# Batch 0's stretch dealt in another order, its squares summed by TensorE, and one projection product moved ahead in the states' layer

## The chip, the cores and the metric

The kernel runs on one core of a Trainium2 chip. The metric is the device time of one launch in microseconds (us), here the median of three runs. Five engines of a core matter: TensorE (PE, with its weight loads PEld), VectorE (DVE), ScalarE (ACT), GpSimd (POOL) and SyncE (SP), which issues the transfers.

## The reference

```python
# x: (8, 8, 512, 64), state: (8, 8, 32, 64), per batch and head
a  = softmax(x @ state.T / 8)          # 512 x 32
xread = a @ state                      # 512 x 64, the tokens' read
a2 = softmax(state @ x.T / 8)          # 32 x 512
sread = a2 @ x                         # 32 x 64, the states' read
y  = concatenate([xread, sread])       # per batch 544 rows of 8 * 64 = 512
xn = y / sqrt(mean(y * y) + 1e-6) * rms_g
g, v = xn @ w_gate, xn @ w_val         # 512 -> 1536
out = (g * sigmoid(g) * v) @ w_out     # 1536 -> 512
```

Over all batches that makes 4096 token rows and 256 state rows. The computation is in 32-bit floats; the weights and `x` arrive as 64-bit values.

## The kernel before

**Stages.** Batch 0 is computed first, in a stretch of its own in which the weights are also converted. Batches 1 to 7 follow in a steady form. At the end the layer is run once more for the 256 state rows of all batches ("the states").

**Tokens and weights.** The tokens' read of a batch is not written out. Because a softmax over 32 states leaves 32 weights per token and head, the kernel keeps those weights (`aT_s`, 128 x 2 x 512) and folds the states into the layer's weights: `own_weights` multiplies the scaled states `stT_g` with `w_m` (gate and value weights) in L454, and ACT copies the result out of PSUM into `v` (L465). The hidden layer of batch 0 is then `aT_s` times `v` (L496), with Silu on ACT (L502) and the gate product on DVE (L506), and the projection is L694. Batches 1 to 7 and the states use a form with seven block products in place of eight (L600 in `hidden_seven`, L754 in `project_seven`), with sums on DVE and POOL.

**Root mean square.** `tokens_read` does compute the read once (L336), for its squares alone: ACT squares four PSUM banks into `sq` (L343), DVE adds the four (L346, three instructions), TensorE sums over the partitions with a vector of ones (L350, four matmuls of one column), DVE adds 1e-6 (`ss`, L354), POOL takes the power -1/2 (`ri`, L254), TensorE spreads it along the rows (L261), and DVE scales `aT_s` by it (L360). Only then can the hidden layer begin. The token softmax before that is on DVE and ACT: transpose L302, maximum L311, subtraction L313, exponential L315, sum, reciprocal and multiplication (L322 to L327), transpose L329. The state softmax and read, `states_read`, is maximum L372, scaling L375, exponential L378, transposes L385, products L397, scaling L404, transpose L408 and a copy into `xsT` (L410).

**Conversion.** The weights are cut into six groups `mp` of three pieces (gate, value, output). Each piece takes three steps on ACT, L199, L201 and L204 (stream `exponents`), and four on DVE, L225, L228, L232 and L237 (stream `values`). Their raw bits come through a ring of four buffers; the intermediate `ex` and `top` have two buffers each.

**What sets the order.** Every part is a generator. PE, DVE and ACT run in the order in which the generators are stepped; SP's transfers and POOL's work are placed by the scheduler. For batch 0's stretch that order is written out as a string, `ORDER`, one letter per step: `a` and `s` are the tokens' and states' read of batch 0, `A` and `S` those of batch 1, `e` and `d` the conversion, `v` the own weights, `h`, `t`, `u` the hidden products, Silu and gate products of batch 0, `p` and `c` its projection and copies out, `k` sums of the output weights, `w` the first own weights of batch 1, `z` a dummy matmul (`keep_awake`, L845). `PERIOD` does the same for batches 1 to 7, and `STATES` for the states. Inside `hidden_seven`, `sums` finishes each group `mp`: three additions (L662), then the gate (states: L671), then for the later groups a sum (L679) and a difference (L682) that `project_seven` needs.

**Buffers.** PSUM has two banks under the name `at`, two under `pv`, two, one and one for `fx`, `fy` and `fz`. The four reads of L336 take both `at` and both `pv` banks.

Of the kernel before, what the change touches and what calls it, by code (L numbers as in the profile page):

```python
# [8 lines left out]
F32 = mybir.dt.float32  # L9
# [3 lines left out]
ALU = mybir.AluOpType  # L13
# [4 lines left out]
P = 128  # L18
# [1 line left out]
W_BUFS = 3  # L20

ORDER = (
    "aaaaaaaaddaaaaaaeaseeaasadsasszzzzzzzzzzzzzzssdsaaaasaeadesaeeazzsdasaaezzzzzzza"
    "deadaaaddeeazzzzsedaadszzzzzadaeedzzvvavdzzadeaAzzzzhdeeddtdAdAAhueheAeedtddphAe"
    "dvdvduvdphedeAedtdhApeehddeuAdddeAhdedvdtudvvpeAAAAdhdAAteAehuhpddephepdeAdAeApA"
    "dteedAAvvveAdpudAAephtdSdhAdphdeAueedhAdeAteudddeeSppAddAAdppAdAdevApvdveehhAdth"
    "AudhpdeddeedeAdteAupvdvdvphedAAtdShhutSAhpukSSSkkkwSwkpSkpwpSSckSScckkpcSwkkkwww"
    "w"
)

PERIOD = (
# [4 lines left out]

STATES = (
    "hyyyyhthyytthhhuuhtuhththhytuuhuuhthuhhtthyuhyyutyhhhuuuttyuhhutyyhhthuhyhuhuttu"
    "yhuhttyuhuhuuhuthhyuthythytuhuuhuhutuuhuuppcpkpcpukkcpkpkpc"
)  # L40


# [1 line left out]
def kernel(  # L44
# [20 lines left out]
    VE, SE, GE, TE = nc.vector, nc.scalar, nc.gpsimd, nc.tensor  # L65
# [5 lines left out]
    NC = S // P  # L71
# [13 lines left out]
    aps = ctx.enter_context(tc.tile_pool(name="aps", bufs=2, space=PSUM))  # L85
# [4 lines left out]
    seven = {}  # L90
# [17 lines left out]
    def load_x(b, *queues):  # L108
        x_sb[b] = two.tile([P, NC, H * D], F32, name="x_b")
        for c in range(NC):  # L110
# [8 lines left out]
    ones = consts.tile([P, 1], F32, name="ones")  # L119
# [3 lines left out]
                     in0=ones.to_broadcast([P, NC]), op=ALU.pow)  # L123
# [9 lines left out]
    hb = consts.tile([P, NM, S], F32, name="hb")  # L133
# [133 lines left out]
    def tokens_read(b):  # L267
        xb, packed = x_sb[b], rows.pop(b)
        stT = two.tile([P, 4, Ns], F32, name="stT")
        stT_g[b] = two.tile([P, 4, Ns], F32, name="stT_g")  # L270
        tp = aps.tile([P, 4, Ns], F32, name="at")
        TE.transpose(out=tp.rearrange("p j n -> p (j n)"),
                     in_=packed.rearrange("p e d -> p (e d)"), identity=ident)
        yield
        VE.tensor_copy(stT, tp)
        yield "step"

        xT = one.tile([P, 4, NC, P], F32, name="xT", tag="xT")
        for c in range(NC):
            tp = aps.tile([P, 4, P], F32, name="at")  # L280
            for j in range(4):
                TE.transpose(out=tp[:, j, :], in_=xb[:, c, P * j:P * j + P], identity=ident)  # L282
            yield
            SE.copy(xT[:, :, c, :], tp)
            yield "step"


        sp = [aps.tile([P, S], F32, name="at") for e in range(2)]
        for j in range(4):
            for e in range(2):  # L290
                TE.matmul(out=sp[e][Ns * j:Ns * j + Ns, :], lhsT=stT[D * e:D * e + D, j, :],  # L291
                          rhs=xT[D * e:D * e + D, j].rearrange("p c t -> p (c t)"),
                          start=True, stop=True)
        yield


        sS = read[b] = two.tile([P, 2, NC, P], F32, name="sS")
        eS = one.tile([P, 2, S // Ns, Ns], F32, name="eS", tag="eS")
        m1 = two.tile([P, 2, S // Ns], F32, name="m1")
        z1 = two.tile([P, 2, S // Ns], F32, name="z1")  # L300
        for e in range(2):
            VE.transpose(out=eS[:, e].rearrange("p k n -> p (k n)"), in_=sp[e])  # L302
            yield
            SE.copy(sS[:, e].rearrange("p c t -> p (c t)"), sp[e])
            yield "step" if e else None

        def along(t, e):
            return t[:, e].unsqueeze(2).to_broadcast([P, S // Ns, Ns])

        for e in range(2):  # L310
            VE.reduce_max(out=m1[:, e], in_=eS[:, e], axis=AXX)  # L311
            yield
            VE.tensor_tensor(out=eS[:, e], in0=eS[:, e], in1=along(m1, e), op=ALU.subtract)  # L313
            yield
            SE.activation(out=eS[:, e], in_=eS[:, e], func=ACTF.Exp, scale=SCALE)  # L315
            yield "step"
        VE.tensor_tensor(out=stT_g[b], in0=stT, in1=rms_g.unsqueeze(2).to_broadcast([P, 4, Ns]),
                         op=ALU.mult)
        yield
        aT_s[b] = two.tile([P, 2, S], F32, name="aT_s")  # L320
        for e in range(2):
            VE.reduce_sum(out=z1[:, e], in_=eS[:, e], axis=AXX)  # L322
            yield
            VE.tensor_scalar(z1[:, e], z1[:, e], 1e-9, None, op0=ALU.add)
            VE.reciprocal(z1[:, e], z1[:, e])
            yield
            VE.tensor_tensor(out=eS[:, e], in0=eS[:, e], in1=along(z1, e), op=ALU.mult)  # L327
            yield
            VE.transpose(out=aT_s[b][:, e], in_=eS[:, e].rearrange("p k n -> p (k n)"))  # L329
            yield "step"  # L330


        reads = [(aps, vps)[j // 2].tile([P, S], F32, name=("at", "pv")[j // 2]) for j in range(4)]
        for j in range(4):
            for e in range(2):
                TE.matmul(out=reads[j][D * e:D * e + D, :],  # L336
                          lhsT=packed[Ns * j:Ns * j + Ns, e, :],
                          rhs=aT_s[b][Ns * j:Ns * j + Ns, e],
                          start=True, stop=True)
        yield  # L340
        sq = one.tile([P, 4, S], F32, name="sq", tag="xT")
        for i, j in enumerate((2, 3, 0, 1)):
            SE.activation(out=sq[:, i, :], in_=reads[j], func=ACTF.Square, scale=DM ** -0.5)  # L343
            yield "step" if i == 3 else None
        for i, j in ((0, 1), (2, 3), (0, 2)):
            VE.tensor_tensor(out=sq[:, i, :], in0=sq[:, i, :], in1=sq[:, j, :], op=ALU.add)  # L346
            yield
        sp = aps.tile([P, NC], F32, name="at")
        for c in range(NC):
            TE.matmul(out=sp[:, c:c + 1], lhsT=sq[:, 0, P * c:P * c + P], rhs=ones,  # L350
                      start=True, stop=True)
        yield
        ss = two.tile([P, NC], F32, name="ss")
        VE.tensor_scalar(ss, sp, 1e-6, None, op0=ALU.add)  # L354
        yield "step"
        ri = mean_root(ss, NC)
        yield
        rp = along_rows(ri, NC)
        yield
        VE.tensor_tensor(out=aT_s[b], in0=aT_s[b],  # L360
                         in1=rp.unsqueeze(1).to_broadcast([P, 2, S]), op=ALU.mult)
        yield "step"
# [75 lines left out]
    HM = NM // 2  # L438
# [151 lines left out]
    def hidden_seven(n, weights, tokens, silu, after=lambda mp: None):  # L590
# [67 lines left out]
        def sums():  # L658
            for mp, q in enumerate(pairs):
                h = hb[:, 2 * mp:2 * mp + 2, 0:n]  # L660
                for to, ps in ((gates(q)[1], "z"), (gates(q)[0], "y"), (q["c"], "x")):
                    VE.tensor_tensor(out=to, in0=to, in1=q[ps][:, :, 0:half], op=ALU.add)  # L662
                    yield
                if not silu:
                    VE.scalar_tensor_tensor(out=h, in0=h, scalar=1.0, op0=ALU.add, op1=ALU.mult,  # L665
                                            in1=q["g"].rearrange("p m c t -> p m (c t)"))
                    yield
                for i, val in ((1, q["c"]), (0, q["x"][:, :, 0:half])):
                    part = h[:, :, half * i:half * i + half]
                    if silu:  # L670
                        VE.tensor_tensor(out=part, in0=part, in1=val, op=ALU.mult)  # L671
                    else:
                        VE.scalar_tensor_tensor(out=part, in0=part, scalar=0.5, in1=val,
                                                op0=ALU.mult, op1=ALU.mult)
                    yield
                if 2 * mp >= HM:
                    k = 2 * mp - HM
                    upper, lower = (hb[:, k:k + 2, half * i:half * i + half] for i in range(2))
                    VE.tensor_tensor(out=seven["s"][:, k:k + 2, 0:half], in0=lower,  # L679
                                     in1=h[:, :, half:n], op=ALU.add)  # L680
                    yield
                    VE.tensor_tensor(out=lower, in0=upper, in1=lower, op=ALU.subtract)  # L682
                    yield

        return products(), copies(), sums()
# [161 lines left out]
            yield  # L847

    def first_of_batch(b):
        for mp in range(2):  # L850
            for part in own_weights(b, mp):
                yield from part
# [32 lines left out]
                            mybir.EngineType.Activation})  # L885
    with tc.manual_schedule(**by_hand):
        for stream in ORDER:
            if stream in "ck" and "s" not in seven:
                early.close()
                open_late()  # L890
                slot_sums(1)
            next(streams[stream])
    assert all(next(stream, done) is done for name, stream in streams.items() if name != "z")
    load_state(2)
# [64 lines left out]
```

## Time and profile before

| | |
|---|---|
| median of three runs | 800.66 us (800.29 to 801.45) |
| the profiled execution | 800.68 us |
| its span | 798.9 us |
| mean granted TensorE clock | 0.997 |
| PE busy | 786.0 us, 98% of the span |
| DVE, ACT, POOL busy | 515.0, 347.0, 179.0 us |
| first hidden matmul of batch 0 (L496) | about 38.2 us from the start |
| first L600 of batch 1's steady part | 143.4 us |

The span runs from the first to the last instruction; about 1.8 us of the execution's time lie around it. The dummy matmuls L845 count as busy PE time, so the page's 98% holds some microseconds in which PE did nothing useful. Times in views of the trace are counted from the start of the span.

### The profile page before, as it was taken

To read this page: it belongs to the slowest core of one execution; us is meant where nothing else is said; L and a number is where in the kernel's file an instruction comes from. 1 tells how busy PE (TensorE), PEld (TensorE's weight loads), DVE (VectorE), ACT (ScalarE), POOL (GpSimd) and SP (SyncE) were. 2 spreads that over 40 slices of the span, in tenths; PEclk is the share of its full clock that TensorE was granted. 3 is DMA by queue.
4 is the path that set the end of the run, shared out by engine and by line. 5 is a ranking of instruction groups with operands and counts; after the bars stand their busy time and mean duration, and the time that the engine had idled before them with its cause. 6 is when DMAs were issued, how large, how long until landed. Compare 5 with 4: busy or idle time off the path is not lost.

```text
span 798.9 us, 12273 instructions
## 1 busy us (share of the span) xinstructions
PE 786.0 (98%) x4902; PEld 605.2 (76%) x4902; DVE 515.0 (64%) x786; ACT 347.0 (43%) x572; POOL 179.0 (22%) x216
## 2 busy tenths in 40 slices
PE   6999999999999999999999999999999999999998
PEld 5643444788778887888778877888788877888996
DVE  4999996688347842786358833785278635881461
ACT  5998864553245323543255314532354324510320
POOL 0000003530154004510433015500451044400000
PEclk9999999999999999999999999999999999999999
DMA  9987746700182007400461018200540024101311
GB/s 285 262 289 287 263 159 186 264 23 14 34 273 106 1 24 218 185 1 16 127 240 44 4 34 283 107 1 14 193 163 2 14 109 181 66 4 43 113 54 28
DMA packets 61593, 94.13 MB, mean 118 GB/s; under 512 B 38752, under 2 KB 46432, under 8 KB 54624
## 3 DMA queue, kind: packets, MB, share of 16 engines
q1 hardware_dynamic: 59360, 92.75, 34.2%
q10 hardware_dynamic: 2176, 0.59, 0.3%
q8 instruction: 39, 0.64, 0.3%
q14 instruction: 18, 0.15, 0.1%
HBM read 78.12 MB, written 15.20 MB: 117 GB/s over the span
## 4 chain that ended last, share of the span: by engine, by line
PE 93%; DVE 5%; issue 0%; DMA 0%; ACT 0%; SPq 0%
PE f L600 37%; PE f L754 35%; PE f L694 5%; PE pv L496 3%; PE at L454 3%; PE pv L454 3%; PE at L282 2%; PE at L291 1%; DVE ex L232 1%; PE at L397 1%; PE at L336 1%; DVE raw L228 1%; PE at L350 1%; PE at L385 1%; DVE w_m L237 1%
## 5 line engine op out<-in xcount | busy, mean ns | idle before, releaser
L754 PE MATMUL f<-wo,hb 128*128 128x256 f32 x540 | 124.2, 382 | 0.4 <-ACT ot L791 0.2
L662 DVE TENSOR_TENSOR g<-g,f 128x512 f32<-128x512 f32 (+1 forms) x96 | 62.8, 654 | 90.1 <-PE f L600 86.6
L600 PE MATMUL f<-aT_s,v 128*128 128x256 f32 x504 | 119.5, 380 | 0.0
L754 PEld LDWEIGHTS f<-wo,hb 128*128 128x128 f32 x540 | 101.4, 190 | 20.1 <-ACT ot L791 6.9
L600 PEld LDWEIGHTS f<-aT_s,v 128*128 128x128 f32 x504 | 93.8, 190 | 17.3 <-issue 5.2
L254 POOL TENSOR_TENSOR ri<-ss,mhalf 128x4 f32<-128x4 f32 x8 | 9.2, 1156 | 361.8 <-DVE ss L354 361.8
L600 PE MATMUL f<-aT_t,vs 128*128 128x256 f32 x336 | 87.2, 382 | 0.0
L754 PE MATMUL f<-wt,hs 128*128 128x256 f32 x360 | 80.4, 379 | 0.0
L653 ACT ACTIVATE hb<-g 128x1024 f32<-128x1024 f32 (+1 forms) x48 | 48.2, 1004 | 63.0 <-DVE g L662 63.0
L754 PEld LDWEIGHTS f<-wt,hs 128*128 128x128 f32 x360 | 68.3, 190 | 9.5 <-issue 0.2
L791 ACT COPY ot<-f 128x256 f32<-128x256 f32 x60 | 21.5, 372 | 122.5 <-PE f L754 122.5
L600 PEld LDWEIGHTS f<-aT_t,vs 128*128 128x128 f32 x336 | 62.6, 190 | 15.1 <-issue 5.9
L665 DVE SCALAR_TENSOR_TENSOR hb<-hb,g 128x1024 f32<-128x1024 f32 x42 | 55.5, 1320 | 7.8 <-ACT hb L653 7.8
L651 ACT COPY g<-f 128x512 f32<-128x512 f32 (+1 forms) x48 | 26.9, 561 | 76.7 <-PE f L600 76.7
L483 POOL TENSOR_TENSOR vs<-v,vs 128x256 f32<-128x256 f32 x42 | 58.3, 1389 | 0.0
L480 POOL TENSOR_TENSOR vs<-v 128x256 f32<-128x256 f32 x42 | 30.5, 727 | 118.6 <-ACT v L465 118.6
L694 PE MATMUL f<-wo,hb 128*128 128x512 f32 x96 | 44.7, 600 | 0.0
L600 PE MATMUL f<-aT_t,v 128*128 128x256 f32 x168 | 43.9, 383 | 0.0
L496 PE MATMUL pv<-aT_s,v 128*128 128x512 f32 x96 | 43.6, 593 | 0.0
L600 PE MATMUL f<-aT_s,vs 128*128 128x256 f32 x168 | 43.1, 379 | 0.0
L754 PE MATMUL f<-wt,hb 128*128 128x256 f32 x180 | 42.6, 386 | 0.0
L754 PE MATMUL f<-wo,hs 128*128 128x256 f32 x180 | 41.6, 382 | 0.0
(131 smaller groups left out, 1263.4 us busy)
## 6 DMA issues: line engine op xcount, KB each, us to landing
w_m<-w_d SPq DMA_DIRECT2D x48, 1024.0 KB, 6.5
x_b<-in_x_dram SPq DMA_DIRECT2D x30, 256.0 KB, 4.6
out_dram<-ot SPq DMA_DIRECT2D x56, 128.0 KB, 1.8
raw<-in_moe_w_val_dram SPq DMA_DIRECT2D x6, 1024.0 KB, 5.1
raw<-in_moe_w_out_dram SPq DMA_DIRECT2D x6, 1024.0 KB, 7.6
w_d<-w_m SPq DMA_DIRECT2D x6, 1024.0 KB, 4.9
raw<-in_moe_w_gate_dram SPq DMA_DIRECT2D x5, 1024.0 KB, 6.4
raw<-in_moe_w_gate_dram SPq DMA_DIRECT2D x2, 512.0 KB, 4.8
```

The lines of the kernel that those rows point to most:

```text
L454: TE.matmul(out=pv[e][Ns * j:Ns * j + Ns, :], lhsT=stT_g[b][D * e:D * e + D, j, :], rhs=w[D * e:D * e + D, j].rearrange("p m k f -> p (m k ...
L480: GE.tensor_tensor(out=vs[:, 0], in0=a21, in1=a22, op=ALU.add)
L483: GE.tensor_tensor(out=vs[:, 2], in0=a12, in1=vs[:, 1], op=ALU.subtract)
L496: TE.matmul(out=to[0], lhsT=lhs(i, k), rhs=r, start=(i == 0), stop=(i == len(rhs) - 1))
L600: TE.matmul(out=ps[:, i, 0:half], lhsT=l[:, i, :], rhs=r, start=(start and i == 0 and k == 0), stop=(k == len(lhs) - 1), skip_group_check= ...
L651: SE.copy(gates(q)[1], q["x"][:, :, 0:half])
L653: SE.activation(out=hb[:, 2 * mp:2 * mp + 2, 0:n].rearrange("p m (c t) -> p m c t", c=2), in_=q["g"][:, :, :, 0:half], func=ACTF.Silu if s ...
L662: VE.tensor_tensor(out=to, in0=to, in1=q[ps][:, :, 0:half], op=ALU.add)
L665: VE.scalar_tensor_tensor(out=h, in0=h, scalar=1.0, op0=ALU.add, op1=ALU.mult, in1=q["g"].rearrange("p m c t -> p m (c t)"))
L694: TE.matmul(out=banks[r], lhsT=hb[:, m, P * r:P * r + P], rhs=wo[:, m, :], start=(m == 0), stop=(m == NM - 1))
L754: TE.matmul(out=banks[name][:, r, :], lhsT=lhs(k)[:, P * r:P * r + P], rhs=rhs(k), start=(start and r == 0 and k == 0), stop=(k == HM - 1) ...
L791: SE.copy(to, banks[name][:, r, :])
```

## The change

The letters of `ORDER` are dealt anew. Batch 0's token softmax is no longer interleaved with the conversion and with the states' read; the states' read of batch 0 moves into the stretch of the hidden layer; there are 31 dummy matmuls in place of 40. For batch 0 alone, the three DVE additions of the squares go, and TensorE multiplies all four banks with the ones, sixteen matmuls that add up in PSUM. The POOL sums of batch 1's token weights (`slot_sums`) are issued at the first step of `first_of_batch`, and the late buffers are opened at the first `c`, `k` or `w`. In `STATES`, the first product of the projection stands ahead of the last hidden product and of the last gate product, and `sums` puts the first sum between the two gate products of a group and no longer behind both. `PERIOD` is not touched.

```diff
 ORDER = (
-    "aaaaaaaaddaaaaaaeaseeaasadsasszzzzzzzzzzzzzzssdsaaaasaeadesaeeazzsdasaaezzzzzzza"
-    "deadaaaddeeazzzzsedaadszzzzzadaeedzzvvavdzzadeaAzzzzhdeeddtdAdAAhueheAeedtddphAe"
...
+    "aaaaaaaaadaedeeaaaaaaaaaaeeaaaaaaeaeaaazzzzzzzzzzzzzzzzzzzzaeaaaeddddaddzzzzaadd"
+    "deedaaadzvdaeevddzzaeavdedzzzAzhdAeAdtheeheuhAdddAdpetAeduedevvdpvepAhdAedteddde"
...
 STATES = (
     "hyyyyhthyytthhhuuhtuhththhytuuhuuhthuhhtthyuhyyutyhhhuuuttyuhhutyyhhthuhyhuhuttu"
-    "yhuhttyuhuhuuhuthhyuthythytuhuuhuhutuuhuuppcpkpcpukkcpkpkpc"
+    "yhuhttyuhuhuuhuthhyuthythytuhuuhuhutuuphuupcpkpcpukkcpkpkpc"
 )
...
-        for i, j in ((0, 1), (2, 3), (0, 2)):
-            VE.tensor_tensor(out=sq[:, i, :], in0=sq[:, i, :], in1=sq[:, j, :], op=ALU.add)
-            yield
+
+        n = 4 if b == 0 else 1
+        if n == 1:
+            for i, j in ((0, 1), (2, 3), (0, 2)):
+                VE.tensor_tensor(out=sq[:, i, :], in0=sq[:, i, :], in1=sq[:, j, :], op=ALU.add)
+                yield
         sp = aps.tile([P, NC], F32, name="at")
-        for c in range(NC):
-            TE.matmul(out=sp[:, c:c + 1], lhsT=sq[:, 0, P * c:P * c + P], rhs=ones,
-                      start=True, stop=True)
-        yield
+        for i in range(n):
+            for c in range(NC):
+                TE.matmul(out=sp[:, c:c + 1], lhsT=sq[:, i, P * c:P * c + P], rhs=ones,
+                          start=(i == 0 and c == 0), stop=(i == n - 1), skip_group_check=True)
+            yield
...
+                steps = [lambda: finish(1, q["c"]), lambda: finish(0, q["x"][:, :, 0:half])]
+                if k >= 0:
+                    steps.insert(1 if silu else 2, first_sum)
+                    steps.append(lambda: VE.tensor_tensor(out=lower, in0=upper, in1=lower,
+                                                          op=ALU.subtract))
+                for step in steps:
+                    step()
                     yield
...
     def first_of_batch(b):
+        slot_sums(b)
+        yield
         for mp in range(2):
...
-            if stream in "ck" and "s" not in seven:
+            if stream in "ckw" and "s" not in seven:
                 early.close()
                 open_late()
-                slot_sums(1)
             next(streams[stream])
```

More of the change, by code (lines that the diff above doesn't have):

```diff
@@ L22 @@
 ORDER = (
-    "aaaaaaaaddaaaaaaeaseeaasadsasszzzzzzzzzzzzzzssdsaaaasaeadesaeeazzsdasaaezzzzzzza"
-    "deadaaaddeeazzzzsedaadszzzzzadaeedzzvvavdzzadeaAzzzzhdeeddtdAdAAhueheAeedtddphAe"
[L25 to L28, printed above, removed]
+    "aaaaaaaaadaedeeaaaaaaaaaaeeaaaaaaeaeaaazzzzzzzzzzzzzzzzzzzzaeaaaeddddaddzzzzaadd"
+    "deedaaadzvdaeevddzzaeavdedzzzAzhdAeAdtheeheuhAdddAdpetAeduedevvdpvepAhdAedteddde"
+    "hAueheddApdddepvevhdddevdtdupeddeAeehAtshppAAdhduhdedddeeAveeApvdpvdstuededAddeh"
+    "htpddehetpuAddshpvdeuAsedvspAAAAApveshAhAsdtAdudedhedsehtAsAApupdeeAedAppddAdAAv"
+    "AedAvAdpAsvAhSSetdhuShAdhtukkAASwsSkwkkwSpSSSSkpcpSkwskkkckSwpcSSscskwwww"
 )
@@ L344, in tokens_read @@
             yield "step" if i == 3 else None
-        for i, j in ((0, 1), (2, 3), (0, 2)):
-            VE.tensor_tensor(out=sq[:, i, :], in0=sq[:, i, :], in1=sq[:, j, :], op=ALU.add)
-            yield
-        sp = aps.tile([P, NC], F32, name="at")
-        for c in range(NC):
-            TE.matmul(out=sp[:, c:c + 1], lhsT=sq[:, 0, P * c:P * c + P], rhs=ones,
-                      start=True, stop=True)
-        yield
+        n = 4 if b == 0 else 1
[3 more added lines that the diff above has]
+                yield
+        sp = aps.tile([P, NC], F32, name="at")
+        for i in range(n):
+            for c in range(NC):
+                TE.matmul(out=sp[:, c:c + 1], lhsT=sq[:, i, P * c:P * c + P], rhs=ones,
+                          start=(i == 0 and c == 0), stop=(i == n - 1), skip_group_check=True)
+            yield
         ss = two.tile([P, NC], F32, name="ss")
@@ L667, in sums, with finish @@
                     yield
-                for i, val in ((1, q["c"]), (0, q["x"][:, :, 0:half])):
+                k = 2 * mp - HM
+                upper, lower = (hb[:, k:k + 2, half * i:half * i + half] if k >= 0 else None
+                                for i in range(2))
+                def finish(i, val):
                     part = h[:, :, half * i:half * i + half]
@@ L674, in sums, with first_sum @@
                                                 op0=ALU.mult, op1=ALU.mult)
-                    yield
-                if 2 * mp >= HM:
-                    k = 2 * mp - HM
-                    upper, lower = (hb[:, k:k + 2, half * i:half * i + half] for i in range(2))
+                def first_sum():
                     VE.tensor_tensor(out=seven["s"][:, k:k + 2, 0:half], in0=lower,
                                      in1=h[:, :, half:n], op=ALU.add)
-                    yield
-                    VE.tensor_tensor(out=lower, in0=upper, in1=lower, op=ALU.subtract)
+                steps = [lambda: finish(1, q["c"]), lambda: finish(0, q["x"][:, :, 0:half])]
[5 more added lines that the diff above has]
+                    step()
                     yield
```

## The prediction

> **What bounds the kernel now.** I read the page's part 4 first, then part 2, then the stretches, then the first 38 us of the chain. Line numbers below are those of the kernel before.
>
> ```profile
> PE 93%; DVE 5%; issue 0%; DMA 0%; ACT 0%; SPq 0%
> PE   6999999999999999999999999999999999999998
> ```
>
> TensorE carries 93% of the chain and is thin in the first fortieth only. Next, its waits over the first 145 us, and the stretches (columns: length; busy time of PE, PEld, DVE, ACT, POOL; clock; DMA share; GB/s):
>
> ```profile
> PE at L272 <- DMA rows<-in_state_dram: 5.9, 1, 5.9
> PE at L350 <- DVE sq L346: 1.0, 1, 1.0
> PE at L291 <- ACT xT L284: 0.7, 1, 0.7
> PE at L454 <- DVE w_m L237: 0.7, 1, 0.7
> ...
> 0.00:38.20 38.20, 30.60 (x230) 22.34 (x231) 27.10 (x48) 27.09 (x38) 3.82 (x12) 0.96 0.97 270
> 38.20:143.40 105.20, 104.49 (x487) 45.73 (x486) 92.18 (x115) 76.63 (x97) 10.55 (x13) 1.00 0.71 242
> ```
>
> From 38.2 to 143.4 (batch 0's hidden layer and projection) PE idles for 0.7 us, all of it the L454 wait: that stretch is as long as its matmuls. Before 38.2 much of PE's 30.6 us is the dummy matmul L845, so busy time says nothing there; what counts is when L360 hands the scaled token weights to the first hidden matmul L496. The chain into it (start, us, what):
>
> ```profile
> 22.87 0.61 DVE eS L327
> 23.48 0.02 issue
> 23.50 0.71 DVE aT_s L329
> ...
> 27.39 0.60 DVE sq L346
> 27.99 1.14 DVE ex L232
> 29.13 0.61 DVE sq L346
> 29.76 0.70 DVE sq L346
> 30.60 1.02 PE at L350 x8
> ...
> 32.59 1.70 PE at L454 x16
> 34.29 2.00 PE f L845 x4
> 36.30 0.47 PE at L261 x4
> 36.80 1.22 DVE aT_s L360
> ```
>
> The softmax ends at 24.21; the adds of the squares lie among weight conversion; and the PE stretch behind runs slowly (L454 1.70, 1.09 elsewhere), because the clock is halved:
>
> ```profile
> 33.00:34.00 1.00, 1.00 (x16) 0.00 (x0) 1.00 (x2) 0.97 (x1) 1.00 (x1) 0.50 1.03 393
> ```
>
> **What the Trainium skill says.** Its page "TensorE: Matmul & The Clock Gate", Part 1, says that the clock falls to half after an idle window of about 3.4 us and recovers after as long a busy one. The trace agrees: PE is 40 to 61% busy from 29 to 31 and at 0.50 from about 32.9 to 36.2 (3.3 us). The same page, LDWEIGHTS, says that a load costs its columns, however narrow the product: the eight 128x1 passes of L350 take 1.02, 0.12 each. "PSUM — Partial Sum Buffer", The four PSUM rules: the start flag clears the written bits of the region and later products overwrite or add by element, so one flag for sixteen products is sound; no run here shows it yet.
>
> **The change, part by part.** The program's order on each engine shows four things.
>
> *Softmax (gain).* The old chain from 12.7 to 24.21 (its lines before those shown) holds ten DVE pieces that are not the token softmax: two maxima of `states_read(0)` (L372, 0.59 each), conversions of 0.60, 0.60, 0.35 and 0.60, and small ones of 0.08, 0.09, 0.17 and 0.30; together 3.97. The new order puts them behind L329. Then two maxima and two subtractions run from 12.71 to 15.4; the exponentials (0.6) fit beside, but for some 0.4 of waiting; and each half needs sum, add, reciprocal, multiply and transpose, about 2.55 (20.95 to 24.21 less the 0.6 and 0.3 between). 15.6 + 2 x 2.55 = 20.7, **3.5 earlier**.
>
> *Squares.* L336 ends 1.2 later as before (21.9), and four ACT squares with one conversion step (1.15) between end at 25.3. The three adds (2.1 of DVE, about 3.7 with the conversions among them) are dropped. In their place come 32 passes instead of 8: 32 x 0.12 = 3.9, twelve products from the third square on (about 23.7, 24 x 0.12 = 2.9) and the last eight passes after, ending near 27.6. The sum's `ss` (L354) is queued on DVE behind the first value piece: the first gate halves end at 24.3, the value piece (four steps, 4.27) at 28.6. So the adds' gain is hidden by that piece. POOL's power, 1.16 to 1.98, ends at 29.9 to 30.8; L261 also needs a copy of the first L454 product (to about 31), and ends by 31.2, or 32.2 at half clock.
>
> *The scaling.* L360 stands on DVE behind one more piece (28.7 + 4.27 = 32.95). That covers L261, the half clock and the power's spread. L360 runs from 33.0 instead of 36.80. The first hidden matmul follows at 34.4 (old: 38.22); one or two dummy passes at half clock can push it to 35.2. I take 34.6: **-3.6** (range -4.0 to -2.8).
>
> *The stretch behind.* Moved into it from the head, where dummies covered them: L385 twice (0.44 each), L397 (64 passes, 1.1), L408 (0.11): **+2.1** of PE in a full stretch. Dropped dummies (40 to 31) gain nothing themselves, being fillers. DVE takes 2.55 of small work, ACT 3.0 (two exponentials at 0.91, two copies at 0.59), table loads counted the same. The L454 stall of 0.69 should go: against L360, I put the five later value pieces at 10.5, 24.4, 40.1, 56.0 and 77.7, and PE's own arrival at their L454 at 11.1, 25.2, 41.3, 57.9 and 78.45: slack 0.6 to 1.9, **-0.7**. At the end batch 1's state transposes take the bank of its scale product and wait for L360's second run, and one L454 waits for copies of `xsT`: **+0.6**, seen nowhere before, from the order alone; 0 to 1.5, as a bank could also be free in time. SP now issues batch 2's tokens behind the states' L397, late in the stretch; they are first used some 20 us into the next, a 256 KB load lands in 4.6, so I cost it at nothing, covered by batch 1's first products. POOL's sums for batch 1 (L518 to L521, 0.73 to 1.2 each) keep their place before the first L600 that needs them: nothing. Start flags and the rest of the weight order: nothing, hidden in the same stretch, 0 to 0.3.
>
> *The end.* The last states' product waits:
>
> ```profile
> 775.41 0.42 DVE L662 TENSOR_TENSOR c<-c,f 128x256 f32<-128x256 f32 x1 [0.47 <-PE f L600]
> 775.88 1.16 PE L600 MATMUL f<-x_t,w_m 128*128 128x128 f32 x8 [0.51 <-DVE c L662]
> 776.88 2.75 PE L754 MATMUL f<-wo,hb 128*128 128x256 f32 x12
> ```
>
> The twelve passes of L754 need the first half's gates only, long done, and move into that 0.51. The next product reads the first sum (L679), now issued between the two finishing multiplies: 775.9 + 2 x 0.42 = 776.8, with PE arriving at about 779. The second multiply, 0.42 after the last product, is read 2.6 later. **-0.5** (-0.5 to 0).
>
> *Sum.* -3.6 + 2.1 - 0.7 + 0.6 - 0.5 = **-2.1**. The profiled execution took 800.68 (span 798.9, 1.8 around it), the median 800.66, the same; so 798.6. What a measurement of this kernel can tell from no change is about 0.2%, 1.6 us.
>
> **The rivals.**
> *Nearly nothing comes through (about 800).* The head's gain is 3.6, but 2.1 of states' work must now be paid in a full stretch; if the half clock reaches the first hidden matmuls (3.3 us at half costs up to 1.6) or the value stall stays (0.7), -2.1 becomes -0.5 or -1.4: about 800. For it: 24 to 28.7 holds 128x1 products and a wait for the value piece, a stretch at least as thin as the old one. Against: L261 has more than a microsecond of cover.
> *Slower: ACT becomes the bound.* Up to the last value piece ACT would work about 74 of 77.7 us, 95%; the page gives 76.63 of 105.2 over the whole stretch. Its queue is in order: a Silu waiting for its gate product holds the conversion step (L204) behind it, then DVE's L232 and L237, then PE's L454. By my walk that step is in places only 0.7 ahead. If each of five value pieces comes one conversion step (1.15) past its slack, PE stalls 5.75 in place of 0.69: -1.4 - 0.69 + 5.75 = +3.7, 804.3. It decides once these stalls pass 3.7 together (-2.1 to +1.6). Against: only one such stall, 0.69, is seen now, though DVE is 88% busy in that stretch (92.18 of 105.2).
> *More (797.0).* No half clock and no new bank waits: -4.0 + 2.1 - 0.7 + 0 - 0.5 = -3.1, or 797.6; with some of the states' work in existing gaps, 797.0.
> *The head's gain is no gain:* had L360 been held by conversion anyway, only the end's -0.5 would be left against 2.1 of added work and 0.6 of new waits: +2.2, 802.9. L360's 0.75 us of idle time before it, with L261 as its releaser, speaks against it.
>
> **How the numbers follow.** Forecast, with the case of more, 0.58; nearly nothing 0.24; slower by ACT 0.12 or by an idle head gain 0.06. The range from 796.8 to 802.0 holds the first two cases and the near part of the slower ones. Chances: faster 0.58, same 0.24, slower 0.18.
>
> **What would show it.** L360 starts near 33.0 and the first L496 at 34.4 to 35.2; `ss` right behind the first value piece; the ones-product group takes about 3.9 in two parts; no PE wait over 0.3 at L454 in mp 1 to 5; the stretch from the first L496 to the steady L600 grows by about 2; the tail's 0.51 is gone. L360 later than 35, or L454 waits of more than 2 together, would make the forecast wrong.

## The result, and the profile after

The changed kernel took 800.88 us (median of four runs, 800.64 to 802.30) against 800.89 before: a ratio (of the means) of 1.0004, 95% interval 0.9986 to 1.0021. A second comparison, of thirteen runs, gave 800.63 against 800.83 and 1.0005 (0.9997 to 1.0013). So the change made no measurable difference, where 2.1 us less had been forecast as likeliest, with 0.58 on faster and 0.24 on no change. The profiled execution has a span of 799.0 us against 798.9.

The page of the changed kernel, the shares of its chain and its slices:

```profile
PE 97%; DVE 2%; DMA 0%; ACT 0%; SPq 0%; issue 0%; DVEq 0%
PE   6999998999999999999999999999999999999998
```

TensorE holds more of the chain than before, 97% in place of 93%. For the head (all that comes before the first hidden product) this says little: the chain runs there through the dummy products, 40 passes of L856 for 10.2 us alone, because TensorE always has one to do. The seventh digit of the PE row has dropped from 9 to 8, a new thin place at 120 to 140 us. From here on the lines are those of the changed kernel: L350 became L353, L360 became L363, L454 became L457, L496 became L499, L600 became L603, and the output weights' sums L735 became L746. TensorE's waits over the first 145 us (total, times, longest):

```profile
PE at L411 <- DVE sr L407: 1.1, 1, 1.1
PE at L388 <- DVE aT_s L363: 0.9, 1, 0.9
```

The two stretches, cut at the first hidden product and at the first steady L603 (columns as for the kernel before):

```profile
0.00:35.70 35.70, 28.98 (x164) 20.84 (x165) 23.81 (x37) 22.60 (x31) 3.23 (x12) 0.95 0.93 257
35.70:144.40 108.70, 106.69 (x560) 47.32 (x559) 96.77 (x123) 80.39 (x105) 12.37 (x13) 1.00 0.70 242
```

The two old waits, for the squares and for the value piece, are gone; those for the first transfer and for the first transposes are left, 6.0 (5.9 before) and 0.7. Two new ones stand at the end of the stretch, and DVE and ACT are busier in it than before. The bookkeeping between the same events in both traces closes:

| stretch | before | after | difference | worked out |
|---|---|---|---|---|
| start to first hidden product (L496, L499) | 38.43 | 35.71 | -2.7 | -3.6 |
| from there to the first steady L600, L603 | 104.99 | 108.66 | +3.7 | +2.0 |
| batches 1 to 7, to the states' last product but one | 630.00 | 629.99 | 0.0 | 0.0 |
| from there to the end of the span | 25.48 | 24.64 | -0.8 | -0.5 |
| span | 798.9 | 799.0 | +0.1 | -2.1 |

So the question is about two places: 0.9 us that the head did not give, and 1.7 us that the stretch took.

**The head.** Its chain in the changed kernel (start, us, what):

```profile
25.78 3.82 PE at L353 x32
29.60 1.06 PE f L856 x2
30.66 1.88 PE at L457 x16
...
33.60 0.44 PE at L260 x4
```

One row of the 1-us windows (the clock is the third number from the end):

```profile
30.00:31.00 1.00, 1.00 (x10) 0.23 (x16) 0.97 (x2) 1.00 (x2) 0.94 (x1) 0.50 0.63 221
```

TensorE never stops here, yet its clock is 0.50: L457 takes 1.88 and two dummy passes 1.06. The half clock lasts from 29.0 to 32.4; it begins 3.3 us after the 32 one-column passes of L353 began. In this execution the start was slow as well: the score products L290 took 1.96 us against 1.09 before, and the softmax ended at 21.95, not at 20.7. The scaling did not wait for TensorE here (L260 ended at 34.04). It followed the output piece on DVE without a stop:

```profile
34.15 1.21 DVE L363 TENSOR_TENSOR aT_s<-aT_s,at 128x1024 f32<-128x1024 f32 x1
```

It starts 1.15 later than worked out (33.0), about as much as the softmax was late (1.25), and the first hidden product 1.1 later (35.71 against 34.6). So in this execution it is the slow start, more than the half clock, that holds the head. Which of the two it is in others is seen below.

**The end of the stretch.** The chain, in which DVE holds 13 us:

```profile
123.59 0.69 DVE hb L509
...
125.61 1.13 DVE aT_s L363
...
134.34 1.10 DVE wt L746
135.44 1.13 DVE wo L746
136.57 0.40 DVE sr L407 x2
```

Two rows of POOL's timeline (start, us, instruction):

```profile
126.87 1.05 POOL L521 TENSOR_TENSOR aT_t<-aT_s 128x256 f32<-128x256 f32 x1 [9.08 <-DVE aT_s L363]
128.00 1.06 POOL L522 TENSOR_TENSOR aT_t<-aT_s,aT_t 128x256 f32<-128x256 f32 x1
```

Batch 1's scaling (L363) now runs at 125.6, behind a gate product and two sums; before, it ran at 122.09. POOL's sums of the token weights, which need it, begin at 126.9 in place of 123.4 and lie on top of the output weights' sums on DVE. There both are slow: the twelve L746 take 11.3 us together (L735 before: 9.2), single ones 1.2 against 0.7, and POOL's sums 1.05 against 0.73. The Trainium skill, "SBUF — State Buffer", SBUF: two separate sides, says that DVE and GpSimd share a port pair that one of them holds for a whole instruction, also for a DVE operation with two inputs in SBUF against a GpSimd operation that reads it. The trace agrees: L746 has two such inputs and takes 0.5 longer where it lies beside a POOL sum. That the order lets them meet is tested below.

### The profile page after: what moved, and what is told of

It reads as the page before. It is cut to its first block, busy times and chain, and to the rows that moved or that the text cites. A ratio compares the mean times of both kernels' runs of the same rounds, so it can differ in the third digit from the quotient of the medians.

```text
span 799.0 us, 12287 instructions
## 1 busy us (share of the span) xinstructions
PE 786.3 (98%) x4908; PEld 605.3 (76%) x4908; DVE 516.0 (65%) x783; ACT 346.0 (43%) x572; POOL 180.1 (23%) x216
## 4 chain that ended last, share of the span: by engine, by line
PE 97%; DVE 2%; DMA 0%; ACT 0%; SPq 0%; issue 0%; DVEq 0%
PE f L603 37%; PE f L765 35%; PE pv L499 5%; PE f L705 4%; PE at L457 3%; PE pv L457 3%; PE f L856 2%; PE at L281 2%; PE at L353 1%; PE at L290 1%; PE at L335 1%; DVE wt L746 1%; PE at L400 1%; PE at L388 1%; DMA rows<-in_state_dram 0%; PE at L260 0%
## 5 line engine op out<-in xcount | busy, mean ns | idle before, releaser
L603 PE MATMUL f<-aT_s,v 128*128 128x256 f32 x504 | 119.7, 381 | 0.0
L603 PEld LDWEIGHTS f<-aT_s,v 128*128 128x128 f32 x504 | 93.7, 190 | 18.2 <-issue 6.1
L603 PE MATMUL f<-aT_t,vs 128*128 128x256 f32 x336 | 87.1, 381 | 0.0
L603 PEld LDWEIGHTS f<-aT_t,vs 128*128 128x128 f32 x336 | 62.7, 190 | 14.3 <-issue 5.0
L654 ACT COPY g<-f 128x512 f32<-128x512 f32 (+1 forms) x48 | 26.8, 559 | 76.7 <-PE f L603 76.7
L603 PE MATMUL f<-aT_t,v 128*128 128x256 f32 x168 | 43.9, 383 | 0.0
L499 PE MATMUL pv<-aT_s,v 128*128 128x512 f32 x96 | 43.6, 595 | 0.0
L603 PE MATMUL f<-aT_s,vs 128*128 128x256 f32 x168 | 43.1, 379 | 0.0
```

The source lines that it names most:

```text
L499: TE.matmul(out=to[0], lhsT=lhs(i, k), rhs=r, start=(i == 0), stop=(i == len(rhs) - 1))
L603: TE.matmul(out=ps[:, i, 0:half], lhsT=l[:, i, :], rhs=r, start=(start and i == 0 and k == 0), stop=(k == len(lhs) - 1), skip_group_check= ...
L654: SE.copy(gates(q)[1], q["x"][:, :, 0:half])
```

## The experiments

All ratios are to runs of the kernel before on the same chip. Its medians on the three chips used are 800.79 to 800.83 us, so near that times from different chips are compared below as well.

**The states' end alone.** The kernel before, with only this and the new order of `sums`:

```diff
-    "yhuhttyuhuhuuhuthhyuthythytuhuuhuhutuuhuuppcpkpcpukkcpkpkpc"
+    "yhuhttyuhuhuuhuthhyuthythytuhuuhuhutuuphuupcpkpcpukkcpkpkpc"
```

> The kernel before, with the change in the states' layer alone (the order string STATES and the order of the sums). If the end is worth what the two traces show, the time from the products ahead of the last one (773.4 in the kernel before) to the end falls by 0.8 us, the 0.51 wait at L600 is gone, and nothing before it moves: 0.5 to 0.8 us less than the kernel before, a ratio of 0.9990 to 0.9994. The rival is that the end's gain depends on the other parts: then the wait comes back at another product and the time is the same. The first 15 us are those of the kernel before, so they are also one more sample of how fast TensorE's clock is there: about 1.1 us for the score products if the fast start is a property of the old order, either 1.1 or 1.9 us if it is chance.

799.97 us, ratio 0.9990 (0.9983 to 0.9996). In TensorE's timeline the first product of the projection follows at 775.27 without a wait, and the next block starts at 778.76:

```profile
773.49 1.95 PE L600 MATMUL f<-xsT,w_m 128*128 128x128 f32 x16
775.27 2.75 PE L762 MATMUL f<-wo,hb 128*128 128x256 f32 x12
...
778.76 0.60 PE L762 MATMUL f<-wt,hs 128*128 128x256 f32 x2
```

From the first of these rows to the last it is 5.27 us; before it was 6.05 (773.42 to 779.47). The end is worth 0.8 by itself. The score products took 1.09 here. The head is that of the kernel before, with a softmax that ends 0.9 later, yet the clock stays at 1.00 in it, where the first trace had 0.50 from 32.8 to 36.2; and the scaling L360, at 36.81 as before, now follows the conversion step without a wait. So the old head's half clock comes in some executions and not in others, and in this one conversion held the scaling, as the last of the prediction's rivals had it.

**Batch 1's scaling early.** The changed kernel, with the power, the spreading and the scaling moved; one letter `w` is dealt a little earlier with them, and TensorE's order behind the scaling stays the same:

```diff
-    ...AedAvAdpAsvAhSSetdhuShAdhtukkAASwsSkw...
+    ...AedAvAdpAsvAAhASSetdAhuShdhtuwkkSsSkw...
```

> The changed kernel, with one edit in ORDER: batch 1's power, its spreading along the rows (L260) and the scaling of its token weights (L363) come about 5 us earlier, ahead of the eleventh gate product and of the first sums of the output weights. Theory: the two new waits (0.92 at L388, 1.05 at L411) have one cause, the late scaling, which also pushes POOL's sums of the token weights (L521 to L524) into the sums of the output weights on DVE (L746), where both run slowly (1.2 in place of 0.7 us). Then both waits go, the twelve L746 take 9 to 10 us together in place of 11.3, and the stretch from the first L499 to the steady L603 shrinks by 1.5 to 2.0 us from 108.5: 1.5 to 2.0 us less than the changed kernel. Rival: DVE is the bound there by its amount of work; then the wait at L411 stays near 1 us, only the 0.92 goes, and the gain is under 1 us. The first 15 us are one more sample of the clock: about 1.9 us for the score products if the slow start belongs to the new order, either value if it is chance.

798.21 us, ratio 0.9971 (0.9960 to 0.9982): 2.4 to 2.7 less than the changed kernel, more than the 1.5 to 2.0 expected. TensorE's waits over the first 145 us are now

```profile
PE at L271 <- DMA rows<-in_state_dram: 5.9, 1, 5.9
PE at L290 <- ACT xT L283: 0.7, 1, 0.7
PE at L457 <- DVE ss L357: 0.3, 1, 0.3
```

and both waits of the stretch's end are gone, though only the scaling was moved and not the instruction that the second one waited for. The twelve L746 take 9.6 us, POOL's first three sums 0.73 each, and the stretch from the first hidden product to the steady L603 is 106.28 (35.76 to 142.04) against 108.66. The rival, that DVE is bound by its amount of work there, falls. The score products took 1.09 and the softmax ended 1 us earlier than in the changed kernel's first profile; but the first hidden product came at 35.76, as late as with the slow start. Here the scaling waits for L260, behind a half clock from 27.4 to 34.2:

```profile
33.90 1.22 DVE L363 TENSOR_TENSOR aT_s<-aT_s,at 128x1024 f32<-128x1024 f32 x1 [0.67 <-PE at L260]
```

So with the slow start DVE's conversion set the scaling, and with the fast one, in this trace, the half clock did; the first hidden product comes at about 35.7 both times.

**The adds on DVE again.**

```diff
-        n = 4 if b == 0 else 1
+        n = 1
```

> The changed kernel, with batch 0's squares added by DVE again (three L348 and four ones-products) at the places in ORDER where the changed kernel issues the extra ones-products. Theory: two adds must wait for the last square at 27.1, with the first value piece queued behind them, so DVE stands still for about 1.5 us and then works 2.1 us more, and the scaling L363 comes 2.5 to 3.5 us later than 34.2; the stretch behind is bound by TensorE and keeps its length, so the kernel is 2.5 to 3.5 us slower than the changed one. Rival: the adds are hidden beside the conversion and POOL's power, and the time differs by less than 1 us. With twelve fewer one-column products TensorE runs dummies for longer, so if one-column products are what halves the clock near 29 us, the half clock goes or shrinks.

804.72 us, ratio 1.0046 (1.0030 to 1.0061), 3.8 more than the changed kernel and a little more than the 2.5 to 3.5 expected. TensorE waits 7.0 us for the last add, the first hidden product comes 4.0 later (39.68), and the stretch behind keeps its length (108.68). Under this order the adds are not hidden; the order was not dealt for them, so this is the price of the adds at these places and not the best that they could do. TensorE stood idle here from 24.15, and its clock fell 2.6 us later, at 26.8; so the question what one-column products do stays open in this run.

**TensorE busy from the start.**

```diff
 ORDER = (
-    "aaaaaaaaadaedee...
+    "zzzzzzaaaaaaaaadaedee...
```

> The changed kernel, with six more dummy products (L856) at the very start, while TensorE waits 6 us for the first states. Theory: what separates the two traces before 13 us (score products 1.96 against 1.09 us, softmax end 1.3 us later than worked out) is the clock's warm-up, which by chance came later in the changed kernel's profile; with TensorE busy from 1.5 us on it is warm when the first transposes start, the scores take 1.1 us, the transposes are shorter too, the first hidden product comes 1.3 to 2 us before 35.7, and the time falls by 0.8 to 2 us below the changed kernel's (less of it where executions start warm anyway). Rival: the slow scores have another cause (the transfer or the banks); then they stay at 1.9 us and nothing moves; or the dummies end after the states have landed and delay the first transpose.

800.38 us, ratio 0.9996 (0.9988 to 1.0004). The scores took 1.09 and the softmax ended at 20.6, yet the first hidden product came at 35.84: the theory's 1.3 to 2 us did not arrive. What held it is in the trace of TensorE:

```profile
28.76 1.96 PE L457 MATMUL at<-w_m,stT_g 64*32 64x512 f32 x16 [0.93 <-DVE ss L357]
30.65 2.07 PE L856 MATMUL f<-ident 128*128 128x256 f32 x4
32.51 1.06 PE L260 MATMUL at<-ident,ri 128*128 128x128 f32 x4
33.37 2.10 PE L856 MATMUL f<-ident 128*128 128x256 f32 x6
```

Half-speed work stands in TensorE's queue in front of L260 and again in front of the first hidden product, and L363 now waits 0.68 for L260. The start's clock is not the lever while this is so.

**The ones 128 columns wide.** This changes nothing but the width of batch 0's products with the ones:

```diff
-        sp = aps.tile([P, NC], F32, name="at")
+        wide = P if b == 0 else 1
+        sp = aps.tile([P, NC, wide], F32, name="at")
...
-                TE.matmul(out=sp[:, c:c + 1], ..., rhs=ones,
+                TE.matmul(out=sp[:, c, :], ..., rhs=ones.to_broadcast([P, wide]),
...
-        VE.tensor_scalar(ss, sp, 1e-6, None, op0=ALU.add)
+        VE.tensor_scalar(ss, sp[:, :, 0], 1e-6, None, op0=ALU.add)
```

> The changed kernel, with batch 0's sixteen products with the ones made 128 columns wide in place of one (the same column 128 times); the sum then reads the first column of each. Number, order and waits of instructions are the same. Theory: in all traces of the new order TensorE's clock falls to half near 28 to 29 us, some 3.3 us after these one-column products begin, although TensorE never stops: products of one column do not count as work. 128 columns take about as long as their weight load (eight passes of L281, 0.86 to 0.95 us, against 0.95 for eight of L353), so the group keeps its 3.7 to 3.9 us; the half clock goes, the first L457 takes 1.1 in place of 1.96 us, L260 ends 1 to 1.5 us earlier against the softmax's end, and the first L499 follows the scaling at once. The time falls by up to 1 us below the changed kernel's: nothing where the start was slow and DVE's output piece sets the scaling, 0.7 to 1 where it was fast. Rival: the clock falls because of TensorE's idle or dummy share before; then L457 still takes 1.96 us and nothing changes.

The group took 3.81 us, as with one column, and the clock stayed full. The same 1-us window:

```profile
30.00:31.00 1.00, 1.00 (x12) 0.74 (x5) 1.00 (x2) 1.00 (x3) 0.46 (x1) 1.00 0.98 393
```

TensorE's timeline:

```profile
29.07 1.09 PE L459 MATMUL at<-w_m,stT_g 64*32 64x512 f32 x16 [0.93 <-DVE ss L359]
...
31.05 0.60 PE L260 MATMUL at<-ident,ri 128*128 128x128 f32 x4
...
34.52 1.98 PE L501 MATMUL pv<-aT_s,v 128*128 128x512 f32 x4 [1.03 <-DVE aT_s L365]
```

The first hidden product comes at 34.52, 1.2 earlier, and now waits for the scaling itself. TensorE even stood still for 0.9 us behind the group, and the clock did not fall. That is the mechanism shown by itself: same instructions, same duration of the group, only the width differs. It is not one execution's luck either: the mean granted clock of all thirteen runs is 1.0, where all seventeen runs of the changed kernel show 0.995 to 0.998. The time was 800.73 us, ratio 0.9996 (0.9988 to 1.0004), not the gain of this profile: its thirteen runs lie at 799.5 to 799.8 or at 800.6 to 800.9. With the half clock gone, the head follows the start again, and I read the two groups as the fast and the slow start. The later kernels, which have the wide ones and dummies at the start, show one group each (the three below: 796.3 to 796.7, 795.8 to 796.4, 799.6 to 800.1), which fits; but no slow execution of the wide ones has a profile, so that is argued, not shown.

**Three edits together,** the early scaling, the wide ones and five dummies at the start:

> The changed kernel with the three edits together: batch 1's scaling early, the ones 128 columns wide, and five dummy products at the very start. Theory: with the clock full from 7 us to the first hidden product the scaling starts right behind the output piece on DVE, near 32.9, the first L499 near 34.3 to 34.6, and the end of the stretch keeps the 2.3 us that the early scaling gave: 1.0 to 1.5 us less than the early scaling alone (798.21), so 796.7 to 797.2. Rival: the conversion on DVE and ACT then bounds the stretch behind; the earlier start comes back as waits of L457 for value pieces (L236), and the time stays within 0.4 of 798.2.

796.57 us, ratio 0.9949 (0.9937 to 0.9962), and all five runs between 796.34 and 796.71. That is 1.6 less than with the early scaling alone (1.0 to 1.5 expected), though the wide ones (800.73) and the dummies at the start (800.38) by themselves had moved nothing clear of the noise. That fits two causes of which each hides what removing the other is worth. The first hidden product is at 33.81 and the steady L605 at 140.21. The rival, a stretch bound by conversion, falls: there is no wait for a value piece.

**Batch 0's scaling ahead of the first output piece's last step, too:**

```diff
-    ...adzvdaeevddzzaeavdedzzzAzh...
+    ...adzvdaevezadaveddedzzAzh...
```

> As the three edits together, with batch 0's scaling (L365 here) ahead of the last conversion step of the first output piece and two dummies fewer. If TensorE bounds the stretch, the first hidden product comes about 1.1 us earlier still, near 33.2, and the time falls by another 0.8 to 1.1 us. If DVE's and ACT's conversion bounds it (the first later value piece was ready about 0.5 us ahead of TensorE in the changed kernel), the earlier start turns into a wait of TensorE for that piece of 0.5 to 1.5 us, and the time is within 0.4 us of the three edits'.

796.08 us, ratio 0.9945 (0.9931 to 0.9958): the best of all, 4.75 less than before. The first hidden product is at 32.16, 1.65 earlier, but only 0.9 of that is left at the steady L605 (139.34) and 0.5 in the time. Waits of 0.2 each appear at a value piece, at a Silu and at a copy, so conversion begins to bind: neither theory's size was quite met.

**The changed kernel once more.**

> The changed kernel, unaltered, once more, for its time in more rounds and a second profile of its head. Theory: the score products L290 take 1.1 or 1.96 us by chance, since TensorE's clock is warm or not when they come, and either way the first L499 starts at 35.7 to 35.9, because the half clock near 29 takes back what a fast start gives; the waits of 0.92 at L388 and 1.05 at L411 are there again. Time 800.3 to 800.9 against 800.8 before. Rival: if the first L499 comes at 34.5 with a fast start, the half clock was not what held it.

800.63 us (ratio above). With a fast start (scores 1.09) the first hidden product came at 35.32, the clock at 0.50 from 26.3 to 33.1, and the scaling waited 0.68 for L260; the waits of 0.9 at L388 and 1.1 at L411 stood there again. So a fast start gives 0.4 in this kernel, a little more than expected, and not the 1.2 that it gains by the softmax's end (20.72 against 21.95).

**The states' read back in the head,** on the kernel with three edits; its steps in `ORDER` stand among the dummies (`s` between the softmax's `a`):

```diff
-    ...aaaaaaaaaaeeaaaaaaeaeaaazzzz...
+    ...aaaaasaaassassaaazzzzzzzzzzzzzzsszsszsszaaasaeeeaeaaazzzz...
```

> The three edits together (796.57), with the states' read of batch 0 put back among the dummies of the head: its maxima, sums and scalings on DVE into and behind the token softmax, its exponentials on ACT between the two of the softmax, its transposes and products on TensorE in place of dummies. Theory: moving that read into the stretch only exchanged two costs. In the head it takes about 2.5 us of DVE (1.36 + 0.16 + 0.34 + 0.46 + 0.29), which is what bounds the head, so the first hidden product comes 2.2 to 2.7 us later than 33.8; the stretch loses the 2.1 us of TensorE work; the time is within 0.6 us of 796.57. Rival: the move was a clear gain, and the kernel is 1.5 us or more slower; or the stretch is bound by DVE, and the lighter stretch gives back more than the head costs.

799.91 us, 3.3 more than with three edits, so it was no even exchange. The first hidden product came 3.6 later (37.42): 2.5 of DVE work and a DVE wait of 0.87 for the states' product in front of the first softmax transpose. The stretch fell by 0.4 only, 106.03 against 106.40, not by 2.1. Where the rest went is seen for the most part. L459 (L457 of the changed kernel) took 2.01 at 125.18 in place of 1.09; by the order its second bank waits for the last gate product, which ends at about 126.0, and the states' product (1.03) had stood in just that gap. Another L459, at 136.35, took 1.54 in place of 1.09, and one at 113.93 waited 0.2 for a value piece. So against these places in the head moving the read was a gain, and it costs the stretch less than its own length.

## Why the prediction was right or wrong

**Right.** The measured time lies within the range, where the rival "nearly nothing comes through" put it, and not where the likeliest case did. That it came to about 800 is in part luck: that rival counted on a half clock that reaches the first hidden products or on the value stall, and neither came; a late head and larger bank waits did, less what the end gave beyond its term. Of the steps, these held. The softmax freed of foreign work ends at 20.6 to 21.1 in the traces of the changed kernel and its single edits that have a fast start (20.7 worked out). The 2.55 for each half in it is what the traces show (2.53 to 2.57), but the sum printed beside it gives 2.36. With a fast start the sum waits behind the first value piece as told (28.5 to 28.8). The ones-products take 3.7 to 4.6 (3.9), the value stall of 0.69 is gone, the stretch without new waits is 106.28 (104.99 + 2.1 - 0.7 makes 106.4), and ACT did not become the bound. SP's later loads cost nothing seen.

**Wrong, the head (-3.6, measured -2.7).** Two steps failed, and either is enough. The first is a term put at nothing: the old trace's fast start was taken for the new kernel ("two maxima and two subtractions run from 12.71 to 15.4"). In its profiled execution they began at 13.96, the softmax ended 1.25 late, and the scaling, behind the output piece on DVE, started at 34.15 and not at 33.0. The second shows where the start is fast: "L261 ... ends by 31.2, or 32.2 at half clock" and, with it, "one or two dummy passes at half clock". The half clock was priced for one matmul group and two passes. It began at 26.3 to 29.0, lasted to between 32.4 and 34.6, and hit everything in TensorE's queue: L457 by 0.9, the dummies between by up to 0.9, L260 by up to 0.5, the dummies behind by up to 0.6. In the early-scaling kernel, with a fast start, L260 ended at 33.9 (32.80 + 1.06), and DVE's cover, to 33.2, was too short. The first hidden product came at 35.3 to 35.8 in four profiles, one with a slow start and three with a fast one; with a fast start and wide ones it came at 34.5, as worked out. The rival "nearly nothing comes through" did name the clock, and the 128x1 products with it; what was set against it, "L261 has more than a microsecond of cover", is the line that failed with a fast start.

**Wrong, the new waits (+0.6, measured 2.0).** The two waits were sized together from the order alone, at 0.6 and at most 1.5. The bank wait came as named, with 0.92. The second was another than the one named: no L457 waits for copies of `xsT`, but L411, the states' last transpose, waits 1.05 for L407 on DVE. The order showed the scaling behind a gate product and two sums; what was missing is that this also moves POOL's four sums onto DVE's twelve, where each slows the other, and so makes L407 late. "POOL's sums for batch 1 (L518 to L521, 0.73 to 1.2 each) keep their place before the first L600 that needs them: nothing" was the wrong line: they kept their place in POOL's order and lost it in time.

**Undersized, the end (-0.5, measured -0.8).** The wait of 0.51 went as told. The rest, 0.27, lay in the run-up around that wait, which a busy queue does not have: 5.27 us are what the 1.79, 2.59 and 0.89 of its products take end to end.

**The states' read (+2.1).** As a sum of its instructions this was right against the stretch without waits, but it is not what putting it elsewhere saves: 0.4 in the run that did so, where gaps opened that it had filled.

## What to carry to other kernels

Moving a producer late on one engine is not priced by its own wait: follow what its consumers on the other engines will then overlap with. Work that keeps an engine "busy" is not work that keeps its clock: when dummies hold the clock of TensorE, real work that is narrow needs the same care, and dummies in the queue ahead of the critical product cost nearly double once the clock has fallen (2.07 in place of 1.13 here). Where two causes each suffice for a delay, removing one shows nothing: remove both before calling either harmless. And work moved off a bound engine into a full one can be cheaper than its length if it lands where that engine would have waited.

## What the runs showed of the hardware

One-column products did not hold TensorE's clock. In the new order it fell to 0.50 between 2.6 and 4.2 us after their start, in four profiles (changed kernel twice, early scaling, dummies at the start), though TensorE was busy without a gap up to the fall; the same group at 128 columns took as long (3.81 us) and kept the clock at 1.00 (mean 1.0 in all thirteen runs). The kernel before, with eight such passes behind a stop of 1.0 us, stands between: 61 of its 77 runs on the three chips have a mean clock of 1.0, the others 0.997 or 0.998. In the 3.41 us ahead of the fall in its first trace TensorE was busy for 2.42, 0.9 of them with one-column passes, so that the prediction's "the trace agrees" with an idle window says too much.

By the clock column of narrow windows, the half clock lasted 3.41 us (kernel before, first profile of the changed kernel), 6.83 (the other three of those profiles) or 10.24 (the adds on DVE): once, twice or three times the same length. The Trainium skill, "TensorE: Matmul & The Clock Gate", Part 1, ties the clock to how busy TensorE is, in a window of about 3.4 us that runs free. The lengths agree with that, and the scatter of the delays fits it; but busy cannot mean instructions in flight. Columns streamed would fit, though only the widths 1 and 128 were compared. A free window would also explain why one program took 1.09 or 1.96 us for the same score products at 10 to 13 us, with a clock recorded as 1.00 in both; no run here shows that cause by itself.
